# Attention and a routed mixture of experts: contiguous DVE row transposes inside the first-layer loops, earlier row fetches, late zero-row copies within DRAM

## The chip, the cores and the metric

The kernel runs on one core of a Trainium2 chip. The core has a tensor engine (TensorE, PE), a vector engine (VectorE, DVE), a scalar engine (ScalarE, ACT), GpSimd (POOL) and SyncE (SP), which here only issues DMAs. DMAs run on queues: SyncE's and ScalarE's own, and POOL's for indirect transfers. The metric is the device time of one execution in microseconds, lower is better.

## The reference

Attention with pooled keys and values, then a routing of every token to one expert of eight. 4608 tokens of 512 features, 8 experts with 1024 hidden units, all float32:

```python
    k_p = k.reshape(B, H, Sp, pool, D).mean(axis=3)     # B=8 H=8 S=576 D=64, pool 8
    v_p = v.reshape(B, H, Sp, pool, D).mean(axis=3)
    scores = scale * np.matmul(q, k_p.transpose(0, 1, 3, 2))
    attn = softmax(scores)
    x = matmul(attn, v_p) transposed to (4608, 512)
...
    e_idx = np.argmax(x @ w_gate, axis=1)
    for e in range(E):
        mask = e_idx == e
        h = np.maximum(x[mask] @ w1[e], 0.0)
        out[mask] = gate_w[mask, None] * eom[mask, e, None] * (h @ w2[e])
```

`gate_w` is the softmax value of the chosen expert, `eom` a sigmoid gate.

## The kernel before

**Attention.** One stage, written with a tile scheduler, walks over 36 tiles of 128 tokens, about 4.1 us each. A plan, `at(step, function)`, says behind which tile each piece of preparation is written: loads of keys, values and queries on SyncE's queue (`load_k` L168, `load_q` L172, `load_v` L176), pooling of keys and values over 8 positions on POOL (L193, L208) and VectorE (L212), then per tile the scores (L251), softmax, products with the values (L279) and the normalisation on VectorE (L295, L301). Instructions of an engine and DMAs of a queue run in the order in which they are written.

**Rows.** Each finished group of four tiles is routed, and POOL scatters its rows (640 floats: 512 features, gate, token number) by an indirect DMA (`place_ids`, L415) into the table `xs` in DRAM, which has one region for each expert. A job reads full tiles counted from the end of a region, so its first tile may begin ahead of the region; for this the 128 rows ahead of each region are zeros, written by `no_rows` (L159): nine DMAs from a buffer of zeros on SyncE's queue, at the steps 3, 4.5, ... 15. The scatters of the tiles already done and these copies write the same table.

**First job.** Three tiles of the first expert are worked on while attention ends. `gather_early` waits for the scatters and gathers three tiles of rows by POOL's indirect DMAs (L425); `turn_x` turns each: four TensorE transposes (L452) into PSUM, a copy to the high half by ScalarE (L454), a subtraction for the low half by VectorE (L455). A string, `TAIL`, then says in which order first layer (`M`, L612), ReLU, low halves, weight splits and second layer (`Y`, L618) are issued.

**Block of experts.** Each engine has its own program with semaphores. All products are made in float32 split into two halves, high and low, with three products for one. A job has three tiles (384 tokens, 96 products in the first layer, L899), two, or one ("single"); there are 16 jobs in this input, 9 of three tiles, 7 of two or one (2 singles), 41 tiles in all. VectorE and ScalarE unroll their programs over the eight experts, with branches for the sizes, TensorE loops. For the next job the rows come by ScalarE's DMAs (`fetch`, L969, once the table of rows is ready) into `xq`; VectorE turns them with 32x32 block transposes into PSUM (`turn`, L1049), ScalarE writes the high half `xh` (L980), VectorE the low half `xl` (L1041). TensorE waits for `xl` before a first layer, and before the last tile of a second layer when the next job has three tiles. L938 is a product without use that TensorE makes behind a single. VectorE also makes the low halves of the weights (`split`, L1060, eight pieces for an expert, ScalarE the high ones, L987), the low halves of the hidden layer (L1091) and the scaled outputs (L1080). The first layer's fourth chunk needs the PSUM buffer of the first, so it waits for the first chunk's low half.

The order on VectorE is that of `body`: the last output, then `choose` (the low halves of the hidden layer, with splits between them), then the turns and low halves for the next job, then the outputs. For the first job of the block, whose first layer ran in the attention stage, `choose` runs only five splits.

## Time and profile before

| What | us |
|---|---|
| median of three runs | 658.24 (656.43 to 662.18) |
| the profiled execution | 657.11 |
| its span in the trace | 655.2 |
| TensorE busy | 594.1 (91%) |
| VectorE busy | 378.0 (58%) |
| ScalarE busy | 262.8 (40%) |
| POOL busy | 231.1 (35%) |

TensorE is busy for most of the span. Attention takes about the first 170 us, the tail of attention with the first job until about 191 us, the block of experts the rest. The chain that ended last says which engine's work set the end; the waits of an engine say what it stood still for.

### The profile page before, as it was taken

The numbers are of one execution on the slowest core, as the hardware profiler recorded it, in microseconds if no ns is written. First come the engines' busy times: TensorE is split into PE (matmuls) and PEld (weight loads), VectorE is DVE, ScalarE is ACT, GpSimd is POOL, SyncE is SP. The second block draws the span as 40 slices with busy tenths as digits, with TensorE's granted clock in tenths as the row PEclk, the third lists the DMA queues.
The fourth block names the chain that finished last, engine by engine and source line by source line (L and its number), as shares of the span: only waits on it lengthen the run. The fifth ranks groups of instructions, "written<-read, shape, count | busy, mean of one in ns | idle before, by whom it ended". The sixth has DMA issues, their size and how long they took to land.

```text
span 655.2 us, 12144 instructions
## 1 busy us (share of the span) xinstructions
PE 594.1 (91%) x3555; PEld 539.9 (82%) x3556; DVE 378.0 (58%) x841; ACT 262.8 (40%) x694; POOL 231.1 (35%) x340
## 2 busy tenths in 40 slices
PE   0999979889895999879969999999999799999996
PEld 0899979779884989769767989989898598989895
DVE  5688689897776433677647534276235824242323
ACT  2788868689325212436333402144022411111110
POOL 3677788854333322134112212312121231203031
PEclk9999999999999899989979999999999989999999
DMA  9889899965556521657745710356204022111212
GB/s 260 271 279 301 280 278 355 342 233 203 177 188 226 176 68 40 211 157 221 228 129 185 228 57 29 88 151 202 71 16 147 31 63 62 44 48 40 53 37 40
DMA packets 49614, 101.75 MB, mean 155 GB/s; under 512 B 6411, under 2 KB 27915, under 8 KB 47744
## 3 DMA queue, kind: packets, MB, share of 16 engines
q1 hardware_dynamic: 19488, 64.87, 31.6%
q0 software_dynamic: 8032, 25.58, 11.4%
q10 hardware_dynamic: 22016, 10.49, 6.3%
q14 instruction: 58, 0.48, 0.2%
q8 instruction: 20, 0.33, 0.2%
HBM read 76.73 MB, written 25.49 MB: 156 GB/s over the span
## 4 chain that ended last, share of the span: by engine, by line
PE 58%; DVE 5%; issue 4%; ACT 1%; DVEq 1%; ACTq 1%; POOL 0%; POOLq 0%
PE p_h L899 32%; PE p_y L880 26%; DVE p_x L1049 1%; DVE p_y L1049 1%; DVE w1b L1060 1%; DVE w2b L1060 1%; ACT w2a L987 0%; ACTq L969 0%; DVE xt L1041 0%; DVE w2a L1060 0%; ACT w2b L987 0%; ACT xt L980 0%; DVEq L1040 0%; DVE q_even L1104 0%; DVE rows L640 0%
## 5 line engine op out<-in xcount | busy, mean ns | idle before, releaser
L995 ACT ACTIVATE ht<-p_h 128x384 fp32r<-128x384 f32 (+1 forms) x104 | 46.9, 451 | 243.9 <-PE p_h L899 239.7
L899 PE MATMUL p_h<-xt,w1b 128*128 128x384 f32 (+1 forms) x736 | 119.7, 324 | 10.4 <-issue 8.9
L899 PEld LDWEIGHTS p_h<-xt,w1b 128*128 128x128 f32 x736 | 118.4, 193 | 12.2 <-issue 9.8
L1210 POOL DMA_INDIRECT out<-rows,dst x41 | 42.4, 1034 | 243.3 <-DVE rows L1080 240.5
L1091 DVE SCALAR_TENSOR_TENSOR ht<-p_h,ht 128x384 fp32r<-128x384 f32 (+1 forms) x104 | 52.6, 505 | 114.1 <-ACT ht L995 114.0
L880 PE MATMUL p_y<-w2b,ht 128*128 128x512 f32 x480 | 113.5, 396 | 0.8 <-DVE xt L1041 0.8
L880 PEld LDWEIGHTS p_y<-w2b,ht 128*128 128x128 f32 x480 | 89.8, 188 | 22.2 <-issue 1.3
L899 PE MATMUL p_h<-xt,w1a 128*128 128x256 f32 (+1 forms) x640 | 98.4, 316 | 8.3 <-DVE xt L1041 6.8
L899 PEld LDWEIGHTS p_h<-xt,w1a 128*128 128x128 f32 x640 | 97.4, 197 | 9.8 <-DVE xt L1041 7.2
L880 PE MATMUL p_y<-w2a,ht 128*128 128x512 f32 x408 | 94.5, 390 | 1.3 <-DVE xt L1041 0.8
L880 PEld LDWEIGHTS p_y<-w2a,ht 128*128 128x128 f32 x408 | 76.1, 188 | 17.6 <-issue 2.1
L1080 DVE TENSOR_SCALAR rows<-p_y,sc 128x512 f32<-128x512 f32 x41 | 30.6, 748 | 96.3 <-PE p_y L880 75.8
L262 ACT ACTIVATE p<-p_h,m 128x72 f32<-128x72 f32 x288 | 72.1, 374 | 24.3 <-DVE m L257 23.9
L279 PE MATMUL p_y<-vbd,pT 128*128 128x162 f32 (+1 forms) x480 | 73.1, 305 | 5.3 <-DVE xg L301 5.3
L279 PEld LDWEIGHTS p_y<-vbd,pT 128*128 128x128 f32 (+1 forms) x480 | 60.7, 179 | 8.0 <-issue 6.0
L1187 POOL DMA_INDIRECT rows<-xs,src x51 | 54.7, 1072 | 25.1 <-POOL src L1183 13.5
L193 POOL TENSOR_TENSOR kq<-kq 128x288 f32<-128x288 f32 (+1 forms) x63 | 40.2, 670 | 24.0 <-DMA kq<-kT 16.9
L415 POOL DMA_INDIRECT xs<-xg,where x36 | 37.1, 1031 | 29.6 <-DVE grec L295 9.6
L251 PE MATMUL p_h<-kbd,q_even 128*128 128x144 f32 (+1 forms) x160 | 29.9, 316 | 15.9 <-DMA q_even<-qT 13.2
L272 ACT ACTIVATE pT<-ptr 128x384 f32<-128x384 f32 x72 | 38.7, 537 | 2.9 <-PE ptr L271 2.7
L251 PEld LDWEIGHTS p_h<-kbd,q_even 128*128 128x128 f32 (+1 forms) x160 | 24.0, 200 | 17.5 <-issue 13.5
L271 PE MATMUL ptr<-ident,p 128*128 128x128 f32 x216 | 36.2, 277 | 0.1
(177 smaller groups left out, 688.4 us busy)
## 6 DMA issues: line engine op xcount, KB each, us to landing
stage<-wst SPq DMA_DIRECT2D x64, 512.0 KB, 4.7
kq<-kT SPq DMA_DIRECT2D x7, 1152.0 KB
rows<-xs ACTq DMA_DIRECT2D x32, 192.0 KB
rows<-v SPq DMA_DIRECT2D x16, 288.0 KB
kq<-qT SPq DMA_DIRECT2D x4, 1152.0 KB
rows<-xs ACTq DMA_DIRECT2D x64, 64.0 KB
q_even<-qT SPq DMA_DIRECT2D x3, 1152.0 KB
xs<-stage SPq DMA_DIRECT2D x9, 320.0 KB
```

What stands on the lines that cost most here:

```text
L193: eng.tensor_tensor(k[:, :, 0:w], k[:, :, 0:w], k[:, :, w:2 * w], op=ALU.add)
L251: nc.tensor.matmul(s[r0:r0 + n, 144 * c:144 * c + 144], q_t[b][:, 2 * a + c, s0:s0 + n], kbd[b % 2][:, 2 * a + c, :], start=True, stop=True)
L262: nc.scalar.activation(pt[i % 3][:, 4 * a + h, 0:KEYS], sv[:, h], AF.Exp, bias=m[:, h:h + 1])
L272: nc.scalar.activation(pT_t[i][:, 3 * a:3 * a + 3, :], tr[:, 0:384].rearrange("p (c n) -> p c n", c=3), AF.Copy)
L279: nc.tensor.matmul(av[r0:r0 + n, COLS * c:COLS * c + 2 * COLS], pT[:, 3 * a + c, r0:r0 + n], vbd[b % 2][:, a, c].rearrange("p h f -> p (h ...
L415: ins = nc.gpsimd.indirect_dma_start(out=whole_rows(xs), out_offset=bass.IndirectOffsetOnAxis(ap=where, axis=0), in_=x.bitcast(I32), in_of ...
L880: i = mm(to, ht[:, h, f, P * k:P * k + P], w[:, part, o:o + DM], start=(f == 0 and part == 0 and h == 0), stop=(f == 7 and h == 1))
L899: i = mm(to, w[:, part, o:o + P], x, start=(d == 0 and k == 0), stop=(d == 3 and k == len(terms) - 1))
L995: act(ht[:, 0, f, 0:size * P], p_h[f % 3][:, 0:size * P], AF.Relu).then_inc(q["hh"], 1)
L1091: nc.vector.scalar_tensor_tensor(ht[:, 1, f, 0:n], src, 0.0, ht[:, 0, f, 0:n].bitcast(F32), op0=ALU.max, op1=ALU.subtract).then_inc(q["hl" ...
L1187: nc.gpsimd.indirect_dma_start(out=xm[:, k].bitcast(I32), out_offset=None, in_=xs, in_offset=bass.IndirectOffsetOnAxis(ap=src[:, k:k + 1], ...
L1210: nc.gpsimd.indirect_dma_start(out=out, out_offset=bass.IndirectOffsetOnAxis(ap=dst[:, k:k + 1], axis=0), in_=yb[2 if k == size - 1 else k ...
```

## The change

1. A turn reads contiguous elements: the order of features inside a row is read as (d r) instead of (r d), and the rows of the first layer's weights are permuted on the host to match.
2. The first job: rows come by five plain DMAs on SyncE's queue (four of 32 partitions into `xq`, one for the gate part), and VectorE's block transposes take the place of TensorE's. Three small VectorE operations for the gather's indices go.
3. In the block the turns stand inside the first-layer loop (behind chunk 4, 5, 6 of a job of three tiles, 5, 6, 7 of a pair), where no weight splits are placed there; else behind the loop. All turns come first, then all low halves. The first job of the block has turns, two splits, low halves, then the other three splits.
4. `fetch` is issued ahead of ScalarE's wait for the row table of the later jobs. A pair's two tiles come by four DMAs, not eight, when their rows are neighbours, else only the first tile comes.
5. Zero rows: one DMA writes them once to DRAM, at step 3; eight copies within DRAM stand at the steps 27 to 34 and wait for no scatter.

```diff
+TURN = {3: 4, 2: 5}
...
     def no_rows(e):
-        ins = nc.sync.dma_start(whole_rows(xs)[e * STRIDE:e * STRIDE + P, :], sh.stage[STAGES - 1][:, 0:ROW].bitcast(I32))
-        tc.add_to_no_dep_group("ids", ins.ins)
+        none = whole_rows(xs)[ZROW:ZROW + P, :]
+        if e == E:
+            nc.sync.dma_start(none, sh.stage[STAGES - 1][:, 0:ROW].bitcast(I32))
+        else:
+            ins = nc.sync.dma_start(whole_rows(xs)[e * STRIDE:e * STRIDE + P, :], none)
+            tc.declare_no_dep(ins.ins, group="placed", reason="these rows take no scattered row")
+            tc.add_to_no_dep_group("ids", ins.ins)
...
-    for e in range(E + 1):
-        at(3 + 1.5 * e, no_rows, e)
+    at(3, no_rows, E)
+    for e in range(E):
+        at(27 + e, no_rows, e)
...
     def gather_early():
...
-        for k in range(WIDE):
-            ins = nc.gpsimd.indirect_dma_start(out=sh.xb[:, k].bitcast(I32), out_offset=None, in_=whole_rows(xs),
-                                               in_offset=bass.IndirectOffsetOnAxis(ap=sh.src[:, k:k + 1], axis=0))
-            tc.add_to_no_dep_group("ids", ins.ins)
+        first_rows = whole_rows(xs)[P:P + WIDE * P, :]
+        moves = [(sh.xq[32 * h:32 * h + 32], first_rows[:, P * h:P * h + P].rearrange("(g t) f -> t g f", t=32)) for h in range(4)]
+        moves.append((sh.xm, first_rows[:, DM:ROW].rearrange("(k p) f -> p k f", p=P)))
+        for to, rows in moves:
+            nc.sync.dma_start(to.bitcast(I32), rows)
...
     def turn_x(k):
-        for c in range(4):
-            nc.tensor.transpose(tr[:, c], features(sh.xb[:, k], c), ident)
+        nc.vector.transpose(tr.rearrange("p d (g t) -> p g d t", g=4), sh.xq[:, 4 * k:4 * k + 4].rearrange("p g (d r) -> p g d r", d=4))
...
+            fetch(u + size, more, q["xd"])
             eng.wait_ge(q["t"], ROWS)
-            fetch(u + size, more, q["xd"])
...
-                                xq[:, 4 * k:4 * k + 4].rearrange("p g (r d) -> p g d r", d=4)).then_inc(q["tx"], 1)
+                                xq[:, 4 * k:4 * k + 4].rearrange("p g (d r) -> p g d r", d=4)).then_inc(q["tx"], 1)
...
             def hidden(some):
                 for f in range(8):
                     low(f, p_h[f % 3][:, 0:n], n)
                     split(some[f:f + 1])
+                    if not some:
+                        turns(u + size, job + 1, more, range(3)[max(f - TURN[size], 0):max(f - TURN[size] + 1, 0)])
                 eng.nop().then_inc(q["ad"], 8)
+                if some:
+                    turns(u + size, job + 1, more, range(3))
+                lows(u + size, more)
...
+            def first_of_all(some):
+                turns(u + size, job + 1, more, range(3), aside)
+                split(some[:2])
+                lows(u + size, more, aside)
+                split(some[2:])
```

**SyncE's queue in attention, before.** A value load, a query load, then zero rows (`xs<-stage`), which wait for scatters (the DMASW semaphores), and behind them a key load:

```order
L176 DMA rows<-v 72x2x512 [waits DMAHW6_49]
L172 DMA kq<-qT 128x2304 [waits DMAHW7_49,PE_49]
L159 DMA xs<-stage 128x640 [waits DMAHW0_49,DMASW1_49,DMASW0_49]
L168 DMA kq<-kT 128x2304 [waits DMAHW1_49,Activation_49]
L159 DMA xs<-stage 128x640 [waits DMAHW2_49,DMASW3_49,DMASW2_49]
L159 DMA xs<-stage 128x640 [waits DMAHW3_49]
L176 DMA rows<-v 72x2x512 [waits DMAHW4_49,DVE_49,Pool_49]
```

After, around the same key load:

```order
L178 DMA rows<-v 8x2x512 [waits DMAHW2_49,Pool_49]
L178 DMA rows<-v 72x2x512 [waits DMAHW3_49]
L174 DMA kq<-qT 128x2304 [waits DMAHW4_49,PE_49]
L170 DMA kq<-kT 128x2304 [waits DMAHW5_49,Activation_49]
L178 DMA rows<-v 72x2x512 [waits DMAHW6_49,DVE_49,Pool_49]
L178 DMA rows<-v 32x2x512 [waits DMAHW7_49]
```

No zero row stands between the query load and the key load any more. Late in attention the queue holds zero-row copies (`xs<-xs`), the first weight loads (`stage<-wst`) and the five fetches of the first job (`rows<-xs`, here the buffers `xq` and `xm`):

```order
L428 DMA stage<-wst 128x1024 [waits DMAHW0_49,DVE_49]
L160 DMA xs<-xs 16x5120 [waits DMAHW1_49]
L428 DMA stage<-wst 128x1024 [waits DMAHW2_49]
L160 DMA xs<-xs 16x5120 [waits DMAHW3_49]
L425 DMA rows<-xs 32x12x128 [waits DMASW4_49,DMASW5_49,DMASW3_49,DMASW6_49,DMASW2_49,DMASW7_49,DMASW1_49,DMAHW4_49,DMASW0_49,Pool_49]
L425 DMA rows<-xs 32x12x128 [waits DMAHW5_49]
L425 DMA rows<-xs 32x12x128 [waits DMAHW6_49]
L425 DMA rows<-xs 32x12x128 [waits DMAHW7_49]
L425 DMA rows<-xs 128x3x128 [waits DMAHW0_49,Pool_49]
```

The first of the five fetches waits for all scatters, and two later entries stand behind it.

**VectorE at the first job's turns, before** (L295 and L301 normalise a tile of attention, L351 to L355 route, L455 is the low half of x):

```order
L455 TENSOR_TENSOR xt<-xtr_2293,xt 128x4x128
L295 RECIPROCAL grec_2224<-p_y 128x4
L347 TENSOR_REDUCE gden_2316<-ex_2228 128x4
L301 TENSOR_TENSOR xg_2222<-p_y,grec_2224 128x320
L351 TENSOR_TENSOR pos_2320<-rk_2310,running 128x32
L352 TENSOR_SCALAR gden_2316<-gden_2316 128x4
L455 TENSOR_TENSOR xt<-xtr_2326,xt 128x4x128
```

After, where L449 is the transpose, L452 the low half, L297 and L303 the normalisation:

```order
L354 TENSOR_SCALAR gden_2311<-gden_2311 128x4
L449 STREAM_TRANSPOSE xtr_2321<-rows 128x4x4x32
L452 TENSOR_TENSOR xt<-xtr_2321,xt 128x4x128
L297 RECIPROCAL grec_2222<-p_y 128x4
L356 TENSOR_TENSOR running<-running,rk_2305 128x8
L357 TENSOR_TENSOR pos_2315<-pos_2315,oh_2248 128x32
L303 TENSOR_TENSOR xg_2220<-p_y,grec_2222 128x320
```

Each low half has now its transpose ahead of it on VectorE, and ScalarE's high half lies between the two.

**VectorE at the first job of the block, before** (L1060 are splits of weights, L1049 turns, L1041 low halves, of which the third stands in a branch):

```order
L1060 TENSOR_TENSOR w1b<-stage,w1b 128x1024 x4
L1060 TENSOR_TENSOR w2b<-stage,w2b 128x1024
L795 UNCONDITIONAL_BRANCH
L1048 ISA
L1049 STREAM_TRANSPOSE p_x<-rows 128x4x4x32 x2
L1040 ISA
L1041 TENSOR_TENSOR xt<-p_x,xt 128x4x128
L1120 ISA
L1120 REGISTER_ALU x2
L1120 COMPARE_AND_BRANCH
L1126 COMPARE_AND_BRANCH
L1049 STREAM_TRANSPOSE p_h<-rows 128x4x4x32
```

After (L1047 turns, L1072 splits, L1039 low halves):

```order
L1047 STREAM_TRANSPOSE p_x<-rows 128x4x4x32 x2
L1059 ISA
L1059 REGISTER_ALU x2
L1059 COMPARE_AND_BRANCH
L1047 STREAM_TRANSPOSE p_h<-rows 128x4x4x32
L1059 UNCONDITIONAL_BRANCH
L1072 TENSOR_TENSOR w1b<-stage,w1b 128x1024 x2
L1038 ISA
L1039 TENSOR_TENSOR xt<-p_x,xt 128x4x128
L1038 REGISTER_ALU
L1039 TENSOR_TENSOR xt<-p_x,xt 128x4x128
L1065 COMPARE_AND_BRANCH
```

The turns moved from behind five splits to ahead of them, and the low halves stand behind two of them.

## Rows read from the trace of the kernel before

**Rows 1.** The page's part 4, the chain that ended last: shares of the span.

```profile
PE 58%; DVE 5%; issue 4%; ACT 1%; DVEq 1%; ACTq 1%; POOL 0%; POOLq 0%
```

**Rows 2.** What TensorE waited for: us in total, times, longest.

```profile
PE p_h L899 <- issue: 8.9, 2, 7.0
...
PE p_h L899 <- DVE xt L1041: 6.8, 1, 6.8
...
PE p_y L938 <- DVE xt L1041: 6.3, 2, 3.3
...
PE p_y L880 <- DVE xt L1041: 1.7, 2, 0.8
```

**Rows 3.** The same view for SyncE's DMA queue.

```profile
SPq L159 <- DMA xs<-xg,where: 21.2, 4, 10.8
```

**Rows 4.** Timeline, 60 to 87 us: start, us, instruction, count, idle before it.

```profile
60.76 0.45 SPq L168 DMA_DIRECT2D kq<-kT  x1
...
69.26 5.73 POOL L193 TENSOR_TENSOR kq<-kq 128x288 f32<-128x288 f32 x9 [6.52 <-ACT p L262]
...
82.38 1.08 DVE L212 TENSOR_TENSOR rows<-rows 128x384 f32<-128x384 f32 x1 [3.06 <-POOL rows L208]
...
85.98 0.79 PE L279 MATMUL p_y<-vbd,pT 128*128 128x162 f32 x4 [3.66 <-DVE xg L301]
```

**Rows 5.** Windows: busy time of each engine (instructions), granted clock, DMA share, GB/s.

```profile
60.00:90.00 30.00, 26.34 (x224) 24.43 (x223) 22.51 (x79) 22.30 (x84) 20.37 (x28) 1.00 0.91 277
131.00:180.00 49.00, 44.91 (x347) 42.20 (x346) 40.51 (x175) 33.60 (x114) 22.98 (x26) 1.00 0.58 204
213.00:229.00 16.00, 16.00 (x83) 16.00 (x82) 8.07 (x12) 4.07 (x8) 5.13 (x8) 0.87 0.57 181
278.00:295.00 17.00, 12.32 (x54) 10.45 (x53) 12.83 (x19) 6.01 (x10) 6.28 (x9) 0.82 0.53 153
```

**Rows 6.** VectorE by form: count, busy us, mean ns of one, idle before.

```profile
L1049 DVE STREAM_TRANSPOSE p_x<-rows 128x512 f32<-128x512 f32 x32 | 33.2, 1086 | 0.0
...
L1041 DVE TENSOR_TENSOR xt<-p_x,xt 128x512 fp32r<-128x512 f32 x32 | 21.6, 676 | 0.7
...
L640 DVE TENSOR_REDUCE rows<-rows 128x100 f32<-128x700 f32 x1 | 1.5, 1481 | 0.0
```

**Rows 7.** Timeline, 159 to 172 us, the first job's preparation.

```profile
167.42 0.72 PE L452 MATMUL xtr<-ident,rows 128*128 128x128 f32 x4 [1.80 <-DMA rows<-xs,src]
...
168.81 0.69 DVE L455 TENSOR_TENSOR xt<-xtr,xt 128x512 fp32r<-128x512 f32 x1 [2.18 <-ACT xt L454]
...
169.52 2.71 PE L612 MATMUL p_h<-xt,w1a 128*128 128x384 f32 x14
```

**Rows 8.** Timeline, 190 to 236 us, entry of the block of experts.

```profile
191.84 0.52 DVE L635 TENSOR_TENSOR rows<-number,upto 128x350 f32<-128x350 f32 x1 [2.47 <-PEq L1275]
...
195.79 0.18 DVE L645 TENSOR_SCALAR ids<-rows 128x50 int32<-128x50 f32 x1
...
196.90 2.85 ACTq L969 DMA_DIRECT2D rows<-xs  x4
...
201.32 4.63 DVE L1060 TENSOR_TENSOR w1b<-stage,w1b 128x1024 fp32r<-128x1024 f32 x4 [5.34 <-ACT w1b L987]
...
207.00 2.04 DVE L1049 STREAM_TRANSPOSE p_x<-rows 128x512 f32<-128x512 f32 x2
...
212.00 19.27 PE L899 MATMUL p_h<-xt,w1a 128*128 128x384 f32 x96 [6.82 <-DVE xt L1041]
...
218.62 0.56 DVE L1091 SCALAR_TENSOR_TENSOR ht<-p_h,ht 128x384 fp32r<-128x384 f32 x1 [0.89 <-ACT ht L995]
```

**Rows 9.** The chain in order of time, two pieces: start, us, what.

```profile
326.23 7.03 issue
...
471.38 16.96 PE p_h L899 x96
```

**Rows 10.** Timeline, 282 to 291 us, behind the first single.

```profile
288.62 0.63 PE L938 MATMUL p_y<-w2b,ht 128*128 128x512 f32 x1 [3.29 <-DVE xt L1041]
```

More of the change, by code (lines that the diff above doesn't have):

```diff
@@ L1054, in turn_and_xl, with turns, lows @@
             xl(u, k, to)
+        def turns(u, job, more, ks, to=None):
+            for k in ks:
+                if k < 2:
+                    turn(u, k, job)
+                else:
+                    with eng.If(more > 0):
+                        turn(u, k, job, to)
+        def lows(u, more, to=None):
+            xl(u, 0)
+            xl(u, 1)
+            with eng.If(more > 0):
+                xl(u, 2, to)
         def split(some):
@@ L1109, in hidden_one @@
                             split(some[POS.index(f - 1):][:1])
+                turns(u + size, job + 1, more, range(3))
+                lows(u + size, more)
+            def first_of_all(some):
[3 more added lines that the diff above has]
+                split(some[2:])
             with eng.If(job > 0):
@@ L1115, in body @@
             done = started(e, size, rows, nth)
-            choose(eng, e, size, single, nth, hidden, hidden_one, split, done, late)
-            turn(u + size, 0, job + 1)
-            turn(u + size, 1, job + 1)
-            xl(u + size, 0)
-            with eng.If(more > 0):
-                if done is None:
-                    turn(u + size, 2, job + 1)
-                    xl(u + size, 1)
-                    xl(u + size, 2)
-                else:
-                    with eng.If(done > 0):
-                        turn(u + size, 2, job + 1, aside)
-                        xl(u + size, 1)
-                        xl(u + size, 2, aside)
-                    with eng.Else():
-                        turn(u + size, 2, job + 1)
-                        xl(u + size, 1)
-                        xl(u + size, 2)
-            with eng.Else():
-                xl(u + size, 1)
+            choose(eng, e, size, single, nth, hidden, hidden_one, first_of_all, done, late)
             rest(eng, e, size, single, nth, split, 0, INIT + 1 if done is not None else 4, done, late)
```

31 lines of the change are left out of this document (12 added, 19 removed).

## The prediction, made before the changed kernel ran

> **What bounds the kernel now.** I read the chain of waits first: TensorE is 58% of it, VectorE 5%, and 4% is time for which the profile shows no wait [rows 1]. So an edit pays only where TensorE stands still, and the list of what TensorE waited for says where [rows 2]: 8.9 us for nothing that is shown (7.0 of it once), 6.8 us once for the low half of x in the block (L1041), 6.3 us in two waits of the dummy product L938 for the same low half, 1.7 us in two waits of L880. All but the first of these end in work that turns rows of x. Next I read what the queues waited for, since a DMA queue can hold up TensorE through two others: SyncE stood 21.2 us, in four waits, at the zero rows (L159) until scatters of POOL had landed [rows 3]. The timeline behind one of them shows what that costs [rows 4]: the key load L168, next in SyncE's queue, leaves only at 60.76; POOL's pooling L193 begins at 69.26 after 6.52 us of idling; POOL is therefore late with the values that VectorE's L212 needs at 82.38 (3.06 us waited), and TensorE stands 3.66 us at 85.98.
>
> **The change part by part.** The sum is made against the profiled execution's own 657.11 us (span 655.2, 1.9 around it); the median of the three runs is 658.24, 0.2% more, so I carry no correction.
>
> *A, zero rows.* Eight of nine copies go from steps 4.5 to 15 to steps 27 to 34 and wait for no scatter; the ninth keeps an early place. Nothing then stands ahead of the key load, which leaves some 6 to 9 us sooner, and POOL with it by its 6.52 us of idling. That removes VectorE's 3.06 us and most of TensorE's 3.66 [rows 4]. I take -3.6. The bounds: -4.5, if smaller waits of the same origin go too, and -2, since the DMA engines are 0.91 busy from 60 to 90 us [rows 5] and an earlier load may only land as fast as they let it. The late copies, 320 KB each, fall where the engines are 0.58 busy [rows 5]: nothing for them, but on the same queue they stand beside the weight loads and the five fetches of B; those stand ahead of two weight loads and wait for the last scatters.
>
> *The price of a turn.* A transpose that reads with a step of four elements takes 1086 ns for 128x512; the subtraction over as many elements, which reads one at a time, 676 ns; the reduction L640, which reads SBUF across rows, 1481 ns for 700 elements [rows 6]. No row shows a transpose with contiguous reads. From above it is bounded by 1.09 (the step costs nothing), from below by the 0.60 to 0.68 of a simple pass; I take 0.70, nearer the subtraction, because the strided reduction is dear per element too. [...]
>
> *B, first job.* Removed: the wait of 1.80 us for the third gather and three groups of four TensorE transposes, 0.72 for the third [rows 7], about 4 us of TensorE if all lay on the path, and three small VectorE operations. Added: three turns of 0.70 on VectorE, each behind the landing, followed in program order by its low half, which waits for ACT. In the old order VectorE reached L455 with 0.69 of work after 2.18 of idling, and the first layer began at 169.52 [rows 7]. In the new, TensorE's values keep passing through VectorE's L301, which now stands in the queue behind turn, ACT's copy (0.67 from the end of TensorE's transposes at 168.14 to L455) and low half: three times 0.70 + 0.67 + 0.69 = 6.2 us of VectorE's queue instead of three low halves and a wait of 2.18 (4.2). The difference, +2.0, lands on the start of the first layer: 171.5. Ends: -1, if the fetch lands early enough that all hides beside the last attention products; +3.1 with turns of 1.09.
>
> *C, entry of the block.* Before: VectorE works on the row table from 191.84 to 195.97, only then does ACT issue its fetch, from 196.90 to 199.75; VectorE makes five splits from 201.32, turns from 207.00, and TensorE, ready at 205.18, starts at 212.00 [rows 8]. After: the fetch precedes ACT's wait for the table. It can leave 0.93 (the gap from table to DMA) behind a start near 191.3, so 192.2 to 195.0. The landing is not shown; it lies between 0 and the 7.25 to the first turn, I take 3. Turns 198.0 to 200.2; two splits of 1.16 (4.63 for four, [rows 8]) to 202.6; three low halves to 204.7. TensorE's 6.82 us go. But three splits and 5.7 us of the old queue (outputs and further splits, from 212.00 until VectorE began the 0.89 of idling ahead of 218.62) now follow the lows: the first low half of the hidden layer comes at 204.7 + 3.5 + 5.7 = 213.9, and the fourth chunk's products need its buffer at 205.2 + 3 x 2.1 = 211.5: a new wait of 2.4, with the low half itself 3.0. The first layer of before took 19.27 for 96 products, in a stretch where the clock was granted at 0.87 [rows 5, 8], against 16.96 [rows 9]; with no idling ahead I take 16.96. End: 205.2 + 17.0 + 3.0 = 225.2 against 231.27, so -6. A part of the slow-clock stretch may stay (2.3 us, a chance of 1 in 5): -5.5. Ends: -7, and -2.4 if the landing takes all 7.25 (turns 4.3 later, TensorE waits 3.7).
>
> *D, the two singles.* TensorE stands 3.29 at 288.62 until the last low half [rows 10], and 3.0 in the other case (6.3 in all, [rows 2]): turn, ACT, low half, three times. With turns of 0.70 the last low half is 0.4 x 2 to 0.4 x 3 sooner, but in the new order (all turns, then all lows) the first low half comes later; I take -0.8 each, -1.6 together. Ends: +1 (turns not faster), -4 (the granted clock stays up behind them).
>
> *E, turns in the loops.* The two waits of L880 for the low half, 1.7 together, go, since the turns are done beside the first layer, where VectorE waits for ACT anyway. Where nothing waits now, the earlier turn is worth nothing: no other row has a wait for it. The fetch before the table's wait and the pair's four DMAs instead of eight change the issue on ACT, off the path: 0.
>
> *G, longer code.* VectorE's static program grows from 2877 to 3637 instructions, since turns and lows now stand in each variant of the loops. At 326.23 the chain holds 7.03 us in which no wait is shown [rows 9], and the unexplained waits of TensorE are 8.9 in all [rows 2]. I take +1, between -1 (the fetch falls elsewhere) and +4.
>
> Sum: -3.6 + 2.0 - 5.5 - 1.6 - 1.7 + 1 = -9.4, so 647.7, told as 648.
>
> **The rivals.** *The turn is not faster (0.20).* For it: the step is only four elements, and half of a turn's price may be the block exchange itself. Then A -3.6, B +3.1, C -4.3 (three turns of 0.39 more), D +1.0, E -0.9 (only the wait whose turns go into a loop), G +1: -3.7, 653.4. *The attention gets nothing (0.10).* The DMA engines are 0.91 busy at 60 to 90 us [rows 5], so an earlier key load may only push the value loads back, and L212 waits for those: the sum without A is -5.8, 651.3. *The clock (0.12).* The stretch of the first single was granted 0.82, that behind the block's entry 0.87 [rows 5]; there it cost 2.3 us of the first layer. If the shorter standstills keep the clock up, as much comes back at each of two singles, and with A at its end (-0.9 more) the time is 642.2. *Slower (0.08).* The longer VectorE program stalls where jobs change. Seven times the expert changes, and VectorE must take a branch over code that was never run; the chain shows such an unexplained stop of 7.03 once [rows 9]. TensorE's two waits of this kind took 7.0 and 1.9; at 3 for each of the seven changes it is 21 us on a sum of -10.4 without G: 667.7. It decides from 1.5 us a change on, where the gain is eaten up. [...] Against it: VectorE idles through most of an expert's second layer, and only one stop of that length is on the chain.
>
> **How the numbers follow.** The forecast has 0.50, with a spread of its own of 644.5 to 652 from the ends of B, C and G. A measurement here cannot tell a change under 1% from none, so faster means below 651.7 and slower above 664.8. Faster: nearly all of the forecast (0.46), the clock's 0.12, half of the attention's case (0.05), a little of the first rival (0.03): 0.66. Slower: 0.08. The rest, 0.26, is within 1%. The range from 641 to 656 holds the forecast, the clock and both middle rivals; left out are the slow case and the far tails, 0.15 to 0.2.
>
> **What would show it.** A: L160's copies after 130 us without a scatter ahead of them, SyncE's wait for scatters gone, L212 no longer waiting for POOL. Turn: STREAM_TRANSPOSE at 0.6 to 0.8 us; at 1.09 the first rival holds. B: the start of the first layer at about 171.6, with VectorE's queue between. C: TensorE idle under 1 us at the block's entry, and a wait for the low half of the hidden layer at its fourth chunk. D: L938 waiting 2.5 instead of 3.3. G: more of the time without a shown cause on TensorE than 8.9 us. The prediction is wrong if the fetch at the block's entry lands late, or if VectorE's queue, which the change fills on the path in B and C, holds up more than the work that it displaces.

## The result: 1.0% faster, and the profile after

| | before | after |
|---|---|---|
| median of 20 runs, us | 658.92 (654.32 to 667.04) | 653.35 (646.74 to 657.56) |
| ratio | 1 | 0.9898, 95% interval 0.987 to 0.9926 |
| profiled execution, us | 657.11 (span 655.2) | 653.54 (span 651.8) |

The median went from 658.92 to 653.35, where 648 was forecast from a profiled execution of 657.11; the range of 641 to 656 holds it. The ratio compares the means of the runs within 1.5% of the fastest of their kernel (18 of 20 before, 16 of 20 after), so it is not the quotient of the two medians (0.9915). The two profiled executions differ by 3.6 us only, so what follows is a balance of 3.4 us of span, and it has large terms of both signs.

What TensorE waited for in the changed kernel (us in total, times, longest; beside [rows 2]):

```profile
PE p_h L895 <- issue: 4.8, 1, 4.8
PE p_y L281 <- DVE xg L303: 4.3, 2, 3.9
PE p_h L895 <- DVE q_even L1121: 3.3, 1, 3.3
PE p_y L934 <- DVE xt L1039: 3.3, 2, 1.9
...
PE p_h L895 <- DVE xt L1039: 2.4, 1, 2.4
...
PE ptr L273 <- DVE xt L452: 2.1, 1, 2.1
```

The waits for the low half of x fell from 6.8 to 2.4 at the block's entry and from 6.3 to 3.3 behind the singles, and L880's 1.7 are gone. Two are new: 3.3 for the sums of a single (L1121) and 2.1 in the first job. The attention's normalisation holds TensorE up as long as before, 3.9 us instead of 3.66 [rows 4], only at another place (127.10 instead of 85.98). SyncE's queue, which stood 21.2 us for scatters at the zero rows [rows 3], stands there 0.2 us for another transfer, and 8.0 for scatters at the first job's fetch:

```profile
SPq L425 <- DMA xs<-xg,where: 8.0, 1, 8.0
...
SPq L160 <- DMA rows<-v: 0.2, 1, 0.2
```

VectorE by form (count, busy us, mean ns): a turn takes 0.71 us where it took 1.09 [rows 6], the low half as long as before.

```profile
L1047 DVE STREAM_TRANSPOSE p_x<-rows 128x512 f32<-128x512 f32 x32 | 22.1, 710 | 7.8 <-DMA rows<-xs 7.8
...
L1039 DVE TENSOR_TENSOR xt<-p_x,xt 128x512 fp32r<-128x512 f32 x32 | 20.5, 680 | 5.2 <-ACT xt L978 5.0
```

The attention, in the timeline (beside [rows 4]): the key load that left at 60.76 leaves at 50.93, and POOL's pooling behind it begins at 63.09 instead of 69.26. But one subtraction of the routing, L325, whose median is 193 ns, takes 4.01 and 4.97 us, each time beside nine additions of POOL's key pooling:

```profile
50.93 0.38 SPq L170 DMA_DIRECT2D kq<-kT  x1
...
63.09 5.86 POOL L195 TENSOR_TENSOR kq<-kq 128x288 f32<-128x288 f32 x9 [0.60 <-DMA kq<-kT]
...
101.02 5.70 POOL L195 TENSOR_TENSOR kq<-kq 128x288 f32<-128x288 f32 x9
...
101.44 4.01 DVE L325 TENSOR_TENSOR d<-lg,mx 128x32 f32<-128x32 f32 x1
...
121.67 4.97 DVE L325 TENSOR_TENSOR d<-lg,mx 128x32 f32<-128x32 f32 x1
...
122.24 5.67 POOL L195 TENSOR_TENSOR kq<-kq 128x288 f32<-128x288 f32 x9
...
127.10 1.99 PE L281 MATMUL p_y<-vbd,pT 128*128 128x162 f32 x6 [3.88 <-DVE xg L303]
```

The first exponential of tile 18 comes 5.2 us sooner than before (82.51 against 87.70), that of tile 22 at 98.67 against 103.91, that of tile 28 at 130.82 against 130.50: the lead is given back beside these two. The kernel before has such stops too, in the same stretch, of other lengths:

```profile
124.42 3.94 POOL L193 TENSOR_TENSOR kq<-kq 128x288 f32<-128x288 f32 x6
124.45 3.12 DVE L327 SCALAR_TENSOR_TENSOR cand<-d,rev 128x32 f32<-128x32 f32 x1
```

The first job and the block's entry, in the timeline of the changed kernel (beside [rows 7, 8]):

```profile
165.97 0.55 PE L273 MATMUL ptr<-ident,p 128*128 128x128 f32 x3 [2.11 <-DVE xt L452]
...
170.80 0.45 PE L608 MATMUL p_h<-xt,w1a 128*128 128x384 f32 x1 [0.27 <-ACT xt L451]
...
171.52 4.76 PE L608 MATMUL p_h<-xt,w1a 128*128 128x384 f32 x17 [0.28 <-DVE xt L452]
...
196.31 3.73 ACTq L964 DMA_DIRECT2D rows<-xs  x4
...
199.16 0.18 DVE L641 TENSOR_SCALAR ids<-rows 128x50 int32<-128x50 f32 x1
...
204.94 1.32 DVE L1047 STREAM_TRANSPOSE p_x<-rows 128x512 f32<-128x512 f32 x2 [5.60 <-DMA rows<-xs]
...
206.76 2.32 DVE L1072 TENSOR_TENSOR w1b<-stage,w1b 128x1024 fp32r<-128x1024 f32 x2
...
210.94 8.08 PE L895 MATMUL p_h<-xt,w1a 128*128 128x384 f32 x36 [2.41 <-DVE xt L1039]
...
220.32 10.70 PE L895 MATMUL p_h<-xt,w1a 128*128 128x384 f32 x60 [1.30 <-DVE ht L1103]
```

The fetch no longer waits for the table, yet VectorE idles 5.60 us for its landing; TensorE waits 2.41 at the entry, and 1.30 more at the fourth chunk. The second single, in the timeline, first of the changed kernel, then of the kernel before:

```profile
499.81 0.64 PE L895 MATMUL p_h<-xt,w1a 128*128 128x256 f32 x4
502.53 0.75 DVE L1092 TENSOR_SCALAR rows<-p_y,sc 128x512 f32<-128x512 f32 x1 [9.76 <-issue]
503.74 1.65 PE L895 MATMUL p_h<-xt,w1a 128*128 128x256 f32 x6 [3.30 <-DVE q_even L1121]
```

```profile
504.96 3.02 PE L899 MATMUL p_h<-xt,w1a 128*128 128x256 f32 x24
506.54 0.75 DVE L1080 TENSOR_SCALAR rows<-p_y,sc 128x512 f32<-128x512 f32 x1 [6.22 <-issue]
```

VectorE stands 9.76 us with no wait shown where it stood 6.22, and TensorE now waits for it. The DMA view of these 9.76 us lists five packets on the queue that it calls instruction (two in the 6.22 us of before); for which engine they are it does not say. Behind TensorE's wait of 3.30 the granted clock is 0.61 from 503.7 to 511.1, where it was 1.00 in the same job before. The two rows, of the DMA view and of the windows:

```profile
q14 instruction: 5, 0.04, 1.7%
...
503.70:511.10 7.40, 7.36 (x40) 7.36 (x41) 4.22 (x12) 2.81 (x7) 1.92 (x5) 0.61 0.10 37
```

For all kernels I divide the span by the start of the first product of a stage in the trace (for the attention, by the first exponential of the last tile). The names in the first column are explained with the experiments. Stretches in us; the last column is the ratio to the kernel before with its interval:

| kernel | attention to last tile | to block's start | to second layer of its first job | to first layer behind single 1 | to second single's first layer | to its second layer | to next first layer | to the end | ratio |
|---|---|---|---|---|---|---|---|---|---|
| before | 157.8 | 33.4 | 39.9 | 59.5 | 214.3 | 8.0 | 10.9 | 131.3 | |
| after | 158.3 | 36.3 | 36.3 | 57.2 | 209.4 | 13.7 | 9.3 | 131.4 | 0.9898 (0.987 to 0.9926) |
| zero_rows_alone | 160.5 | 32.9 | 39.5 | 60.3 | 213.8 | 8.4 | 10.9 | 130.1 | 0.9988 (0.9951 to 1.0024) |
| splits_first | 159.5 | 34.8 | 32.8 | 57.5 | 210.8 | 14.3 | 9.3 | 131.5 | 0.992 (0.9884 to 0.9957) |
| fetch_behind_wait | 160.7 | 34.9 | 37.8 | 59.6 | 211.5 | 15.0 | 9.4 | 131.3 | 0.9949 (0.9913 to 0.9985) |
| first_lows_later | 162.8 | 35.1 | 36.9 | 57.9 | 211.1 | 14.4 | 9.2 | 130.9 | 0.9968 (0.9931 to 1.0005) |
| turns_once | 157.5 | 36.3 | 34.7 | 62.0 | 210.0 | 7.7 | 9.7 | 130.2 | 0.9849 (0.9816 to 0.9881) |
| turns_behind | 156.7 | 34.9 | 36.2 | 60.0 | 209.8 | 14.4 | 9.7 | 131.1 | 0.9942 (0.9914 to 0.9971) |
| pool_gaps | 159.1 | 36.3 | 36.6 | 57.6 | 211.3 | 14.6 | 9.3 | 131.8 | 0.9971 (0.9943 to 0.9999) |
| stepped_reads | 160.8 | 37.5 | 37.5 | 61.0 | 211.6 | 13.9 | 10.5 | 130.6 | 1.0027 (0.9997 to 1.0058) |
| once_splits | 156.6 | 34.8 | 32.9 | 58.3 | 209.2 | 7.7 | 9.7 | 131.0 | 0.9786 (0.9738 to 0.9834) |
| once_splits_shift | 153.5 | 38.2 | 33.0 | 59.0 | 211.0 | 7.7 | 9.7 | 131.2 | 0.9843 (0.9787 to 0.9899) |
| once_splits_route | 149.8 | 37.4 | 33.0 | 58.4 | 211.3 | 7.7 | 9.7 | 131.3 | 0.9708 (0.9664 to 0.9752) |
| once_splits_zeros_early | 160.0 | 34.8 | 32.9 | 58.1 | 211.2 | 7.7 | 9.7 | 132.0 | 0.9799 (0.9736 to 0.9862) |

Runs of one kernel spread by up to 2%, so a ratio tells the total and a stretch tells the place. Two cautions. The changed kernel was not measured again beside the later ones (each ratio is to the kernel before, measured beside it), and six of the seven kernels made from it by one edit lie above its 0.9898, so a difference of half a percent from that number says little. And a stretch comes from one profile: nine kernels of the table have the same attention up to its last tile (all from the changed kernel except pool_gaps, once_splits_route and once_splits_zeros_early), and take 153.5 to 162.8 us for it.

### The profile page after: what moved, and what is told of

It reads as the page before. It is cut to its first block, busy times and chain, and to the rows that moved or that the text cites. A ratio compares the mean times of both kernels' runs of the same rounds, so it can differ in the third digit from the quotient of the medians.

```text
span 651.8 us, 12082 instructions
## 1 busy us (share of the span) xinstructions
PE 597.1 (92%) x3543; PEld 543.6 (83%) x3544; DVE 367.5 (56%) x840; ACT 260.2 (40%) x694; POOL 228.2 (35%) x337
## 4 chain that ended last, share of the span: by engine, by line
PE 59%; issue 4%; DVE 2%; DMA 2%; ACTq 1%; ACT 1%; DVEq 1%; POOL 0%; POOLq 0%
PE p_h L895 31%; PE p_y L876 28%; DMA rows<-xs 1%; ACTq L964 1%; DMA stage<-wst 1%; DVE w2b L1072 0%; DVE p_x L1047 0%; DVE w2a L1072 0%; ACT w2b L985 0%; ACT w2a L985 0%; DVE q_even L1121 0%; DVE w1b L1072 0%; DVE ht L1103 0%; ACTq L957 0%; POOL out L1216 0%
## 5 line engine op out<-in xcount | busy, mean ns | idle before, releaser
L281 PEld LDWEIGHTS p_y<-vbd,pT 128*128 128x128 f32 (+1 forms) x480 | 62.0, 183 | 10.5 <-issue 5.4
L1193 POOL DMA_INDIRECT rows<-xs,src x51 | 53.9, 1057 | 24.6 <-POOL src L1189 14.3
```

The source lines that it names most:

```text
L281: nc.tensor.matmul(av[r0:r0 + n, COLS * c:COLS * c + 2 * COLS], pT[:, 3 * a + c, r0:r0 + n], vbd[b % 2][:, a, c].rearrange("p h f -> p (h ...
L1193: nc.gpsimd.indirect_dma_start(out=xm[:, k].bitcast(I32), out_offset=None, in_=xs, in_offset=bass.IndirectOffsetOnAxis(ap=src[:, k:k + 1], ...
```

## The experiments

**The zero rows alone**, on the kernel before: its `no_rows` and its two lines of the plan, as in the diff above, and nothing else.

> The kernel before with the zero rows of the changed kernel and nothing else. Theory (the gain is made and then given back): by tile 18 the attention is 5 to 6 us ahead of the kernel before, as in the changed kernel, and between tiles 22 and 28 VectorE's routing instructions with two SBUF operands stand behind POOL's pooling of keys (one of 0.19 us taking 3 to 5 us), so that the first layer begins within 2 us of 169.5; total 656 to 660, no difference. Rival (the late copies cost the gain through the DMA engines): no VectorE instruction is stretched over 2 us in that stretch, and the loss shows as waits for loads of keys, values or weights. Second rival (the loss belongs to the first job's new transposes): the lead of 5 us is kept to tile 35 and the total is near 653.

Measured 0.9988 (0.9951 to 1.0024): nothing that can be told from no change. The attention's last tile begins at 160.5, later than before. The stop stood elsewhere than expected, near tile 15, beside POOL's pooling of values, in the timeline of this kernel:

```profile
74.29 4.11 POOL L213 TENSOR_TENSOR rows<-rows 128x256 f32<-128x256 f32 x6
...
75.19 3.27 DVE L340 TENSOR_TENSOR zs<-lg,oh 128x32 f32<-128x32 f32 x1
...
79.17 1.08 PE L284 MATMUL p_y<-vbd,pT 128*64 128x162 f32 x6 [3.91 <-DVE vbd L244]
```

Further ones of 1.8, 1.5 and 2.0 us follow at 109 to 130. The expected lead at tile 18 was not there (88.76 against 87.70 before): this stop came before it. That a routing instruction stands beside POOL was borne out, its place was not. The first rival falls, since instructions of VectorE are stretched over 2 us, and the second, since no first-job transposes are in this kernel.

**The routing moved.** On the kernel with both edits (below):

```diff
-        at(sum(GROUPS[:g + 1]) + 2, lambda g: queue.append([route(g), 0, g]), g)
+        at(sum(GROUPS[:g + 1]) + 2 + 1.5 * (g in (4, 5)), lambda g: queue.append([route(g), 0, g]), g)
```

> As the one with both edits, with the routing of the groups 4 and 5 written 1.5 steps later, so that its VectorE instructions no longer meet POOL's key pooling at the steps 21.5 and 26. Theory (VectorE's routing instructions stand behind POOL's pooling, and this eats the gain of the zero rows): no routing instruction above 1 us between 100 and 131 us, the attention's last tile 3 to 5 us sooner. Rival (the collisions only move to the next instruction with two SBUF operands, a weight split or the pooling of values): a stretched instruction of 2 us or more stands somewhere else in the stretch and the last tile begins within 1.5 us of the other kernel.

0.9708 against 0.9786, and 641.12 against 645.22 us at the median; all six runs (638.45 to 641.30) are below all six of the other kernel (641.77 to 648.40). The last tile begins at 149.8 instead of 156.6. All occurrences of the subtraction, without and with the move (count, then minimum, median and maximum in ns):

```profile
L325 DVE TENSOR_TENSOR d<-lg,mx x9: 181/242/4000, 43.5 to 172.6; 128x32 f32<-128x32 f32 x9
```

```profile
L325 DVE TENSOR_TENSOR d<-lg,mx x9: 162/191/551, 42.4 to 168.4; 128x32 f32<-128x32 f32 x9
```

No instruction of VectorE's routing takes over 0.75 us between 100 and 131 us any more; the only one over 2 us left is at 66.7. The theory holds, and its size is larger than the 3 to 5 us expected: 6.8. That the stops set the pace there is seen over all fourteen profiles: from tile 22 to tile 28 the attention takes 22.8 us with the routing moved, 26.6 to 27.6 where the longest stretched instruction of VectorE takes 2.0 to 3.1 us (the kernel before is one of these), 28.2 to 30.1 with one of 3.8 to 5.0, and 32.2 in the changed kernel with its two. So these stops were a loss of the kernel before as well. Moving the routing was tried with the late zero rows only. Of the 6.8 us 2.6 are lost again before the block's start (37.4 against 34.8), since TensorE, being early, waits 4.7 instead of 2.1 us in the first job for a turn whose fetch has not landed.

**Gaps in POOL's pooling.**

```diff
                 eng.tensor_tensor(k[:, :, 0:w], k[:, :, 0:w], k[:, :, w:2 * w], op=ALU.add)
+                if eng is nc.gpsimd:
+                    eng.memset(gap, 0.0)
```

> The changed kernel with a small memset on POOL behind each of its pooling additions, so that POOL doesn't read SBUF without a break for 5.7 us. Theory (VectorE's instructions with two SBUF operands get no turn between POOL's additions, as they follow one another without a gap): no routing instruction of VectorE takes over 1.5 us, and the attention's last tile begins 3 to 6 us sooner than with the 4 to 5 us stops, near 153 to 155 us; 648 to 650 in all. Rival (VectorE waits for the end of the whole sequence, whatever is between): instructions of 3 to 5 us remain, and POOL gets slower by its memsets; no gain.

0.9971, no gain on the changed kernel, rather a loss (0.9943 is the lower end of its interval, 0.9926 the upper end of the other). One stop of 3.78 us remains, the others are at 1.6 or below: half the theory, half the rival. Whether a gap of another kind would end the stops was not tried.

**The zero rows early again**, on the kernel with both edits: `no_rows` and the plan of the kernel before.

> As the one with both edits, with the zero rows as in the kernel before. Theory (moving the zero rows brings nothing in the end, since what SyncE's queue gains is given back to the collisions): within 0.3% of the kernel with both edits, with SyncE waiting some 20 us for scatters again and tile 18 some 5 us later than at best. Rival (the zero rows are worth the 3.6 us of the prediction): 0.4 to 0.7% slower.

0.9799 against 0.9786: within 0.3%, as expected, with SyncE waiting 21.6 us for scatters again. As the intervals are 1% wide, a gain of half a percent from the zero rows isn't excluded by this pair; that alone they bring 3.6 us isn't shown by any run. The lead at tile 18 was expected at some 5 us and is 0.5 (84.84 against 85.36). The timelines of this pair, which differs in the zero rows only, first with the late ones, then with the early ones:

```profile
53.67 0.38 SPq L170 DMA_DIRECT2D kq<-kT  x1
66.09 5.73 POOL L195 TENSOR_TENSOR kq<-kq 128x288 f32<-128x288 f32 x9 [3.35 <-ACT pT L274]
```

```profile
60.01 0.39 SPq L165 DMA_DIRECT2D kq<-kT  x1
66.92 5.72 POOL L190 TENSOR_TENSOR kq<-kq 128x288 f32<-128x288 f32 x9 [4.29 <-ACT p L259]
```

The key load leaves 6.3 us sooner and POOL begins 0.8 sooner. At the last tile the two are 3.4 us apart (156.6 against 160.0), the size of the prediction, but 2.9 of it come behind tile 18, when the last early zero row has left the queue (81.32), and profiles with one and the same attention differ by 9. From 55 to 65 us the DMA share with the late zero rows is 1.01 in this pair and 0.83 in the changed kernel; that the DMA engines held the pooling back, as the prediction's second rival has it, is not shown. In the changed kernel and in zero_rows_alone POOL began 6 us and more ahead of the kernel before (63.09 and 62.62 against 69.26).

**Turns once** behind the choice of the loop, as the kernel before has them, so that VectorE's program has 2630 rows instead of 3243 (2636 before, as its listing counts them). The turns and low halves leave `hidden`, `hidden_one` and `first_of_all`:

```diff
+            choose(eng, e, size, single, nth, hidden, hidden_one, split, done, late)
+            if done is None:
+                turns(u + size, job + 1, more, range(3))
+                lows(u + size, more)
+            else:
+                with eng.If(done > 0):
+                    turns(u + size, job + 1, more, range(3), aside)
+                    lows(u + size, more, aside)
...
```

> The changed kernel with turns and low halves once for each job behind the choice of the loop, as in the kernel before (all else changed: contiguous reads, the earlier fetch, the first job, the zero rows); VectorE's program is as short as before, and the five splits at the block's entry stand ahead of the turns again. Theory (the longer VectorE program costs 5.7 to 7 us where the second single begins, since every copy of the loop carries its own turns): from the start of its first layer to its second layer this stretch takes 8 us again, as in the kernel before, instead of 13.7; the two waits of L880 for the low half come back in part (turns of 0.70 instead of 1.09, so below 0.5 each). 3 to 5 us less than the changed kernel. Rival (the stop there comes from TensorE's or ScalarE's program or from where the pages lie): the stretch stays above 12 us.

0.9849 against the changed kernel's 0.9898. The second single's stretch is 7.7 us, and VectorE waits there for TensorE and not the other way, in the timeline of this kernel:

```profile
500.45 7.83 PE L895 MATMUL p_h<-xt,w1a 128*128 128x256 f32 x64
500.65 0.75 DVE L1092 TENSOR_SCALAR rows<-p_y,sc 128x512 f32<-128x512 f32 x1 [4.85 <-PE p_y L876]
```

The waits of L880 did not come back: with turns of 0.71 the turns need no place inside the loops. But of the 6.0 us won at the second single 4.8 are lost up to the first layer behind the first one (62.0 against 57.2): there TensorE stops for 3.32 us with no wait shown instead of 0.86, and the granted clock behind it is 0.64.

**Turns behind the loops, in each copy**, so that the program stays long (3225 rows).

```diff
-                    if not some:
-                        turns(u + size, job + 1, more, range(3)[max(f - TURN[size], 0):max(f - TURN[size] + 1, 0)])
                 eng.nop().then_inc(q["ad"], 8)
-                if some:
-                    turns(u + size, job + 1, more, range(3))
+                turns(u + size, job + 1, more, range(3))
```

> The changed kernel with the turns always behind the loop, but still in each copy of it: the VectorE program is nearly as long as in the changed kernel (18 rows of 3243 less). Theory of length: the stop at the second single stays (13 us or more from its first layer to its second), and the waits of L880 return at below 0.5 each; the time is within 2 us of the changed kernel. Rival (the turns' place inside the loops, not the length, causes the stop): the stretch takes 8 us again.

The stretch takes 14.4 us. In all, seven kernels with the long program need 13.7 to 15.0 there, and seven with the short one 7.7 to 8.4: so the long program goes with the stop, whatever the place of the turns. A program made longer by other rows was not tried, so length by itself is not shown apart from the copies that make it. In total it is 0.9942, more than the 2 us expected above the changed kernel. VectorE's idling without a shown wait is 11.41 us, 9.76 in the changed kernel.

**Three splits ahead of the turns** at the block's entry:

```diff
             def first_of_all(some):
+                split(some[:3])
                 turns(u + size, job + 1, more, range(3), aside)
-                split(some[:2])
                 lows(u + size, more, aside)
-                split(some[2:])
+                split(some[3:])
```

> The changed kernel with three weight splits ahead of the turns at the block's entry, in place of two behind them. Theory (VectorE idled 5.6 us at 204.9 for the late fetch, and the splits then stand on the path between turns and low halves and ahead of the hidden layer's low halves): the splits run in that idle time, TensorE's wait of 2.4 us at the entry falls below 1 us and the one of 1.3 us at the fourth chunk goes; 2.5 to 4 us less, about 650. Rival (the entry is bound by the landing of the fetch alone): the wait stays above 2 us and the time at 652 to 655.

From the block's start to the second layer 32.8 instead of 36.3 us, 3.5 less. The splits run while the fetch lands, and TensorE starts without a wait for x, in the timeline of this kernel:

```profile
201.36 3.50 DVE L1072 TENSOR_TENSOR w1b<-stage,w1b 128x1024 fp32r<-128x1024 f32 x3 [2.26 <-ACT w1b L985]
...
204.77 1.31 DVE L1047 STREAM_TRANSPOSE p_x<-rows 128x512 f32<-128x512 f32 x2
...
208.50 6.52 PE L895 MATMUL p_h<-xt,w1a 128*128 128x384 f32 x36 [0.24 <-issue]
...
216.62 5.67 PE L895 MATMUL p_h<-xt,w1a 128*128 128x384 f32 x31 [1.60 <-DVE ht L1103]
```

The wait at the fourth chunk did not go, it is 1.60. The total, 0.992, is not below the changed kernel's 0.9898 within the intervals; the gain of the stretch is shown by the profile only.

**The fetch behind the wait** for the table again, two lines exchanged.

> The changed kernel with the fetch behind the wait for the row table again. In the changed kernel the first fetch left at 196.31 and the table was done at 199.34. Theory: the fetch leaves 3 to 4 us later, the turns begin 3 to 4 us later and TensorE's wait at the block's entry grows from 2.4 to 5 to 6 us; 656 to 657. Rival (the fetch's landing is set by the traffic of the weight loads beside it, not by its issue): the landing comes at most 1 us later and the time stays within 1 us of the changed kernel.

In total 0.9949. The first DMA leaves 5.7 us after the block's start instead of 1.7, 4.0 later; the turns begin only 1.4 later (11.8 against 10.4), TensorE's wait grows from 2.41 to 3.85. Between both: of four microseconds of earlier issue a third reaches the landing, which leaves room for the rival's cause, traffic beside it, but does not show it.

**The first job's low halves later.**

```diff
         at(36 + 0.5 * k, turn_x, k)
+        at(36.5 + 0.5 * k, low_x, k)
```

> The changed kernel with the low half of each tile of the first job half a step behind its transpose, so that VectorE does a piece of attention while ScalarE writes the high half. Theory (the first job costs 2 to 3 us because VectorE waits 0.66 us for ScalarE three times, with attention queued behind): these waits fall under 0.2 us, TensorE's waits of 2.1 and 1.3 us in this stretch get shorter by 1 to 2 us in all, and the first layer begins 1 to 2 us sooner; 651.5 to 652.5. Rival (the first job is bound by the landing of its fetch and by TensorE's own work): no change of the first layer's start over 0.5 us.

The low half of a tile stands half a step of attention behind its turn, VectorE's waits for ScalarE are gone, and nothing is won: TensorE's 2.1 us stay, and from the last tile to the first layer (its second product, the first that needs a low half) it is 13.1 us against 13.3. In total 0.9968. The theory falls. **The turns half a step later**, on the kernel with both edits:

```diff
-        at(36 + 0.5 * k, turn_x, k)
+        at(36.5 + 0.5 * k, turn_x, k)
```

> As the one with both edits, with the first job's turns half a step later. Theory (TensorE's wait of 2.1 us in the first job is for a PSUM buffer: the turn holds one of the attention's buffers from its place in the order on, while its fetch has not landed; the low half frees it): with the turn half a step later TensorE makes its attention products first, the 2.1 us go, and the first layer begins 0.5 to 1.5 us sooner. Rival (the first layer's start hangs on the chain fetch, three turns, three low halves, whatever stands between): TensorE's wait only moves to the first layer, no gain, or up to 2 us later.

The 2.1 us of TensorE's buffer go, as expected, and a wait of 3.5 us at the first layer takes their place; from the last tile to the first layer 14.5 instead of 13.3. The rival holds: the chain of landing, three turns and three halves sets the start.

**Stepped reads.** The turns read "(r d)" again, the weights' rows lie as before.

> The changed kernel with the turns reading with a step of four elements again, and the weights' rows in the old order. Theory (contiguous reads make a turn 0.70 instead of 1.09 us, but the turns lie on the path only in the first job, at the block's entry and behind the two singles): the transpose takes 1.05 to 1.12 us; the first layer of the first job begins 0.4 to 1.2 us later, the entry 0.8 to 1.2 later, L938's place 0.8 to 1.2 later at each single: 3 to 4 us more than the changed kernel. Rival (turns are hidden beside the loops and waits nearly everywhere): less than 1 us more.

1.0027 (0.9997 to 1.0058) against 0.9898: by these ratios contiguous reads are worth 1.3%, 8.5 us, more than the 3 to 4 expected; against turns_behind (0.9942), which was measured beside it, 0.85%, 5.6 us. By stretches: 1.2 at the first layer of the first job (14.4 against 13.3, three times the 0.38 of a turn), 1.2 up to the second layer of the block's first job, 1.2 behind the second single, 3.8 up to the first layer behind the first single, of which 1.1 are between the single's second layer and the next first layer, and 1.5 at the single's own first layer, where turns_once, turns_behind and fetch_behind_wait have such a loss too. The attention's 2.5 come ahead of the first turn and are not the edit's. So 4.7 are the turns', and the rest is open.

**Both edits**, turns once and three splits ahead of the turns.

> The two edits that the runs so far bear out, together: turns and low halves once behind the choice of the loop (short VectorE program), and at the block's entry three splits, then turns, low halves and two splits. Theory (their gains lie in different stretches and add): the stretch from the second single's first layer to its second takes 8 us, TensorE's wait at the entry is below 1 us; 0.978 to 0.984 of the kernel before, where turns once alone gave 0.985. Rival (the two overlap, since turns once has five splits ahead of the turns already): 0.984 to 0.987.

0.9786 (0.9738 to 0.9834), 645.22 us: the stretches of both show at once, 32.9 and 7.7. Against turns_once (34.7 there, since its five splits run ahead of the turns too) 1.8 us are won at the entry, and 3.7 behind the first single (58.3 against 62.0), which neither edit aims at; so the total lies where the theory has it, but that the two gains add is not shown. With the moved routing it is 0.9708 (641.12 us), the fastest of all, and faster than both kernels of the comparison.

## Why the prediction was right, and where not

The sign and the range held; the sum, -9.4, was too large by 2.7 against the ratio (1.02% of 658.92 is 6.7 us) and by 6.0 against the profiled pair. That the total came so near is in part luck: a term that was not there and others that were too small or too large made up for one another. The measured median is also the first rival's 653.4, though its condition, a turn of 1.09, did not hold. Term by term, in the profiled pair:

| term | predicted | measured | from |
|---|---|---|---|
| A zero rows | -3.6 | +0.4 | attention to last tile |
| B first job | +2.0 | +2.9 | last tile to block's start |
| C entry | -5.5 | -3.6 | block's start to second layer |
| D singles | -1.6 | -3.0 | second layer to next first layer, -1.35 and -1.7 |
| E turns in loops | -1.7 | -1.8 | two jobs of two tiles with the first layer behind |
| G code | +1 | +2.5 | -1.0, -2.2, and +5.7 at the second single |

The remaining -0.8 us are about what the first layer behind the first single gained: 18.27 us instead of 19.23, at a granted clock of 0.92 instead of 0.87.

*A* is the step that failed. Its start was right: the key load left 9.8 us sooner, POOL's pooling began 6.2 sooner, and VectorE's long wait for POOL went. Wrong was the step from there to TensorE, -3.6: the zero rows alone gave 0.9988, and the end of that interval, 0.9951, is a gain of 3.2 us; with both edits they brought 0.5 us at tile 18, and 0.13% in the total; and TensorE's wait for the normalisation only changed its place, 3.9 us at 127.10 for 3.66 at 85.98. The lead of 5.2 us at tile 18 in the profiled pair is not shown to come from the zero rows either: with the same attention and late zero rows tile 18 begins anywhere from 82.51 to 91.61 us, at 87.70 in the kernel before, and at 85.36 in once_splits_zeros_early. The second rival, that the attention gets nothing, had 0.10 and is nearer to what the runs show, though a gain of some us is not excluded; without A the sum is -5.8. What does hold the attention up, in the kernel before too, is stretched instructions of VectorE, of the routing above all, beside POOL's pooling: the prediction asked what is late next on queues and engines, and not what runs at the same time. Moving the routing by 1.5 steps gave 6.8 us of attention. The stretched instructions shown above (L325, in the kernel before L327, in zero_rows_alone L340) have all their operands in SBUF, while L303, which reads PSUM too, stays at 0.48 to 0.49 in all its 72 instances. The stops are longer than one of POOL's additions (0.48 to 0.81 here): those of 4.01 and 4.97 us end 0.1 us after the eighth of the nine has begun. What stretches the instructions is not shown by these runs.

*B*: the first layer was forecast for 171.5; its first product began at 170.80, and its second, which needs a low half, at 171.52. This agreement is luck: 171.5 is 169.52 + 2.0 and leaves out A's -3.6, which did not come. From the last tile to the second product it was 1.3 later than before, not 2.0: the turns' chain behind the landing. VectorE's waits for ScalarE have no part in it, as first_lows_later shows. The other 1.6 us of the stretch's 2.9 go with a lower granted clock, 0.91 from 170 to 190 us here, against 1.00 in the kernel before and in splits_first, whose stretch is 34.8, after the same two waits of 2.1 and 1.3 us. The row of the changed kernel:

```profile
170.00:190.00 20.00, 19.45 (x106) 18.64 (x106) 16.36 (x74) 8.05 (x14) 8.73 (x8) 0.91 0.59 189
```

*C*: the order of events was as written, the landing mis-sized. The first DMA left 1.7 us after the block's start, not 0.9, and VectorE's first turn came 10.4 after the start, not 6.7; from the end of the four issues to that turn it was 4.9 us, not the 3 that were taken. The two splits between turns and low halves then stood on the path: splits_first shows 3.5 us. The wait at the fourth chunk was forecast at 2.4 to 3.0, and was 1.30. The first layer was put down at 17.0 us beside that wait, from a piece at a granted clock of 1.00 [rows 9]; it took 18.6 at a granted clock of 0.91, so the slow stretch, which had a chance of 1 in 5, stayed in large part.

*The turn* was forecast at 0.70 and took 0.71, so the first rival falls; *D* is larger than forecast: it was put low for the order of all turns and then all low halves, and that order costs nothing there, as stepped_reads has it too and with turns of 1.09 is still 0.2 to 0.4 us ahead of the kernel before behind each single. *E* has the right size, but the place in the loops was not needed for it: turns_once, which has no turns in the loops, keeps it, and stepped_reads, with turns of 1.09 in the loops, keeps 0.6 of the 1.7 us of waits. So the shorter turn is enough, and the place alone is not.

*G* had the right sign; the sum missed that the stop falls where nothing covers it, and that the granted clock is 0.61 behind it: of the 5.7 us at the second single 3.3 are TensorE's wait, the rest slower products. Seven changes of expert were feared at 3 us each; there is one such place, and elsewhere stops even became shorter (7.03 to 4.83 [rows 9]). Why that one shortened is open. The stop at the second single goes with the long program, and five packets come in during it on the queue that the DMA view calls instruction; that VectorE waits for them is not shown.

## What to carry to other kernels

When a change lets an engine start earlier, look in the trace for an instruction that is ten times its own median (here 4.01 and 4.97 us against 0.193): something holds it up that no wait names, and the gain may end there. A lead seen in one pair of profiles is not yet the gain of an edit; look whether other kernels with the same code have it. Code copied into each branch of a loop went here with 5.7 us more at a place where nothing covered the stop; make an instruction cheaper first (a turn went from 1.09 to 0.71 us), and then ask whether it still needs a hidden place. Where an engine idles for a landing (5.60 us here), work that needs no landing belongs ahead of the work that does (3.5 us less in the stretch of splits_first).

## What the runs showed of the hardware

- A VectorE instruction with a median of 0.193 us took up to 4.97 us in the changed kernel beside nine POOL additions that followed one another in 5.7 us, and with a small memset between them (pool_gaps) one of 3.78 us was left.
- A 32x32 block transpose of 128x512 floats took 0.71 us with contiguous reads (changed kernel) and 1.09 with a step of 16 bytes (kernel before).
- With VectorE's program of 3243 instead of 2636 rows (as its listing counts them) one place took 5.7 us longer (seven kernels with the long program 13.7 to 15.0 us, seven with the short one 7.7 to 8.4); at the other places no such loss was seen.
- After TensorE had stood for 3.30 us in the changed kernel the granted clock of the next 7.4 us was 0.61 (turns_once: 3.32 us, then 0.64 for 7.8 us); the same job ran at 1.00 in the kernel before, where this stop was missing.
